# Attention and routed experts: k^T v turned once beside its logits' columns with orders made for it, and the second expert's second lot gathered in quarters and turned on VectorE

## The chip, the core and the metric

The kernel runs on one core of one Trainium2 chip. The metric is the device time of one execution in microseconds (us). A core has five engines that the text names: PE (TensorE, matrix products; its weight loads are listed as PEld), DVE (VectorE), ACT (ScalarE), POOL (GpSimd), and SP (SyncE, which here only issues transfers). Each engine works through its own instructions in order. 16 DMA engines move the data.

## What is computed

Linear attention per head, a norm over each head's 64 values, and then a mixture of 8 experts in which each token goes to one. B = H = 8, S = 576 tokens, D = 64, so 4608 tokens of 512 values; each expert has 1024 hidden values. All in fp32.

```python
kv  = einsum('bhsd,bhse->bhde', k, v)            # 64 x 64 per batch and head
out = einsum('bhsd,bhde->bhse', q, kv)
x   = out / sqrt(mean(out*out, -1) + 1e-6) * g_norm      # then B, S, 512
logits = x @ w_gate;  local = sigmoid(x @ w_local)
for each batch b, token s:
    e = argmax(logits[b, s]) if s == 0 or local[b, s] < 0.5 else prev_e
    prev_e = e
    p = exp(logits - max) / (sum + 1e-9)
    y[b, s] = p[e] * (relu(x[b, s] @ w1[e]) @ w2[e])
```

A token's expert can so depend on the token before it, and how many tokens an expert has is known only on the chip.

## The kernel before

**Attention part.** 16 steps, four groups of two batches by four pairs of heads. Step i loads q, forms q times kv for its pair (`q_kv`, L456), forms k^T v for step i+2 (`kv`, L375), and prepares the operand for step i+1. The numbers x have three users: the experts, the norm's sums, and the routing logits. The logits are not taken from x: kv times the gate's weights (9 columns a head: 8 experts and the local gate) is appended to kv, so that one product gives the 64 outputs and the 9 logits of a head. For that, k^T v has to be turned (`turn_kv`, L406), multiplied by the gate's weights `gw` (`logits_of`, L422) and copied in beside kv. Tiles: `kvp` is a pair's k^T v, copied out of PSUM by ACT; `kq` is its turned form; `kvb` is the operand for q, a block for each head laid beside a block of zeros, written by four POOL copies of 64x128 (`kvb_of`, L396) and, for the logits, by two ACT copies. The raw outputs (`raw`, 128x584 a chunk) are stored to a DRAM tile `xs` in rows of four quarters: 128 values, two reciprocal norms and the routing numbers, 146 in each.

A step's work is written as letters that a loop turns into code: `STEP` for the ordinary step and `LATE` for the last three. Q and R are the parts of `q_kv`, K and k those of `kv` of step i+2, V is `turn_kv` of step i+2, L and l the product and copy of the logits of step i+1, 0 and 1 the `kvb` copies, T and U the turns of q, a and c the copies of `raw`, x y X Y the squares for the norm, s the sums, o the store of a chunk (with a weight load in the steps of `LOADED`), w and v the split of a weight (steps of `SPLIT`), e the loads of q. `SLOTS` and `PASS` place the pieces of the routing among them. Inside these parts the order on PE, ACT, DVE and POOL is the order of the code.

**Precision.** Products of the experts are made from numbers split in two: a high part (`w_..h`, `xh`, `hh`) by ACT, a rest (`w_..l`, `xl`, `hl`) by DVE, and three matmuls. A weight tile `wst` (512 KB, four buffers) is loaded by SP (`wfetch`, issued at L186), split by `wsplit` (ACT L233, where the norm's weight is multiplied in, then DVE L234), and the split's end issues the load of the next one in the list.

**Experts.** They are ranked by how many tokens they have. Rank 0 is worked in four blocks of 128 tokens; its fourth block (`block(...)`, L1351) has the splits of rank 1's four w1 tiles (`split`, `w_4` to `w_7`) at its hooks 2, 4, 7 and 8, among its own relu (L1075) and casts (L1082) on ACT. Behind it follow the scales (`scale`, L808) and turns of rank 1's first lot. Ranks 1 to 7 have room for 768, 704, 640, 608, 608, 576 and 512 tokens, each in two lots: `la` of 384 and `lb` of the rest. A lot's first layer is `first_wide` (PE ph, ACT hh L1031, DVE hl L1032), its second is `second` by blocks of 128 (PE py, ACT ot L996, and a POOL scatter of the results at L997).

**Two ways to gather.** Rank 1 fetches each block of 128 tokens with one indirect transfer of whole rows (`gather`, L770, index tile `gidr`), scales it on DVE and turns it on PE (`turn`, L820, four transposes, with an ACT cast and a DVE subtraction behind, L824 and L825). Ranks 2 to 7 fetch a block with four indirect transfers of a quarter row each (`gather4`, L780, index tile `gid4`), partition quarter by partition quarter in such a way that 32x32 transposes on DVE (`turn4`, L797, with L801 and L802 behind) are enough. The rows of w1 then have to be loaded in the order of the quarters (`quarters` in `wfetch`, `gq` in place of `gcol` in the split), which `e > 1` chooses:

```python
if i < NW1 and quarters:
    fetch(t, w1[e].rearrange("o (q j i) f -> j (o q) i f", j=NP, i=QD)[i])
elif i < NW1:
    fetch(t, w1[e, i * P:(i + 1) * P, :].rearrange("o p f -> (o p) f"))
```

The lots' gathers are issued on POOL one after another in the order of the code: rank 1's second lot behind the fourth block's scatter (L1369, `lb`), those of a later lot by `tick` between the products of the lot before it.

Of the kernel before, what the change touches and what calls it, by code (L numbers as in the profile page):

```python
# [22 lines left out]
def kernel(  # L23
# [12 lines left out]
    nc = tc.nc  # L36
# [73 lines left out]
    gid4 = const.tile([P, NP, NR * KBM - KBM], I32, name="gid4")  # L110
# [89 lines left out]
    def wload(e, i):  # L200
        t = wpools["w"].tile([P, 2 * DM], F32, name="wst", bufs=4)
        wfetch(t, by[e], i, e > 1)
        staged[e, i] = t
# [36 lines left out]
    def wsplit(e, i, two=False):  # L240
# [9 lines left out]
        low_ = split_w(hi, lo, t, i, e > 1)  # L250
# [115 lines left out]
    def kv(s):  # L366


        pk = ps_o.tile([P, 2, 512], F32, name="po")
        ks, vs = ([t.pop((s, b)) for b in range(2)] for t in (kts, vts))  # L370
        for c in range(C):
            cd = slice(c * D, (c + 1) * D)
            for b in range(2):
                for x in range(2):
                    nc.tensor.matmul(pk[half(x ^ b), x, 0:D], ks[b][half(x), cd],  # L375
                                     vs[b][half(x), cd], start=(c == 0), stop=(c == C - 1))
        yield
        kvps[s] = wk.tile([P, 2, D], F32, name="kvp")
        nc.scalar.copy(kvps[s], pk[:, :, 0:D])  # L379
        yield  # L380
# [10 lines left out]
    def kvb_of(s, t):  # L391

        if s not in kvbs:
            kvbs[s] = wk.tile([P, 2 * HW + 2 * (HW + D)], F32, name="kvb", bufs=3)
        for y in range(2):
            copy[KVB[t]](pair(kvbs[s][half(t)], slot(0, y) + XO, slot(1, 1 - y), D),  # L396
                         kvps[s][half(y)])
# [3 lines left out]
    def turn_kv(s):  # L401

        pt = ps_q.tile([P, 2, P], F32, name="pt", tag="pq")
        kvp = kvps[s].rearrange("p x d -> p (x d)")
        for t in range(2):
            nc.tensor.transpose(pt[:, 0:2, half(t)], kvp, ident)  # L406
        kqs[s] = wk.tile([P, 2, P], F32, name="kq", bufs=3)
# [10 lines left out]
    def logits_of(s):  # L418

        pm = ps_q.tile([P, 2, 2 * NG], F32, name="pm", tag="pq")  # L420
        for y in range(2):
            nc.tensor.matmul(pm[:, y], kqs[s][:, y], gw[:, s % NP], start=True, stop=True)  # L422
        yield
        for y in range(2):
            copy[LGC](pair(kvbs[s], slot(0, y), slot(1, 1 - y) + D, NG),
                      pm[:, y].rearrange("p (x e) -> p x e", x=2))
# [223 lines left out]
    def by_quarter():  # L650

        n = NR * KBM - KBM
        pq4 = rbank[:, 128:128 + NP * n].rearrange("p (u n) -> p u n", n=n)
        for u in range(NP):
            nc.tensor.matmul(pq4[:, u], sel[0][:, u], trs[0][:, KBM:], start=True, stop=True)
# [122 lines left out]
    def gather4(xr, c, u):  # L778
# [4 lines left out]
            in_offset=bass.IndirectOffsetOnAxis(ap=gid4[:, u, c - KBM:c - KBM + 1], axis=0),  # L783
# [31 lines left out]
    def turn(xr, xh, xl, t0, psum, tag="pt", pin=False, late=False):  # L815

        pt = psum.tile([P, ND, P], F32, name="pt", tag=tag)
        xv = pieces(xr)
# [21 lines left out]
    LOADED = {i: j for j, i in enumerate((0, 1, 2, 3, 5, 10, 13, 14))}  # L840
    SPLIT = {i: j for j, i in enumerate((2, 4, 6, 8, 11, 12, 15))}

    STEP = "Q0saKcwkopRTq1vLlYVmUxeb"
    LATE = {NST - 3: "QKsw1vqkcabLRpo0mlGTVYXUe", NST - 2: "QcmKkLpTRoUea20qlV13xbsy", NST - 1: "45sQRwvacOyX"}

    SLOTS = {}
    for g in range(NGRP - 1):
        for x, what in enumerate("m pqb mb qq p qq".split()
                                 if g < NGRP - 2 else "q . pppmm".split()):
# [9 lines left out]
    def work_of(i, what):  # L859
# [14 lines left out]
        elif what == "R" and now:  # L874
            next(step["c"])
        elif what in "ac" and now:
            next(step[what])
# [261 lines left out]
    PASS = dict(at.split(":") for at in "a0:22o2 a2:s a4:223 a6:3 b1:33t b3:o c3:3x c4:3 c6:T3 d0:3z d5:3 d6:3f d7:r3 d11:3 d15:yF3l".split())  # L1139
# [153 lines left out]

    class Block:
# [17 lines left out]
        def scale(self):  # L1312
            scale(self.xr)
# [10 lines left out]
        def turn(self, xh, xl, t0):  # L1324
            if self.whole:
                turn(self.xr, xh, xl, t0, ps_t)
# [6 lines left out]
    def parts(r):  # L1333
# [3 lines left out]
        bl = [Block(r, k, min(P, n - k * P), r == 1) for k in range(-(-n // P))]  # L1337
# [30 lines left out]
    with tc.manual_schedule(engines=order):  # L1368
        for bl in lb:  # L1369
            bl.gather()  # L1370
# [92 lines left out]
```

## Time and profile before

| what | value |
|---|---|
| median of 3 timed runs | 580.54 us (579.57 to 580.59) |
| profiled execution, its own time | 575.91 us |
| its span, from first to last instruction | 574.1 us |
| DMA traffic | 94.96 MB, 165 GB/s over the span |
| mean granted clock of TensorE | 0.98 |
| largest group on POOL, the quarter gathers (L780) | 120, 133.5 us busy, 1112 ns each |
| weight loads on SP (512 KB each) | 64, median 3.7 us from issue to landing |
| whole-row gathers of rank 1 (L770, `gidr`) | 6, median 6.6 us from issue to landing |

The profile is of one execution. Its busy times are averages over very different parts: attention with the transfers of q, k, v and `xs`, about 9 to 124 us; the four blocks of rank 0, about 124 to 178 us; then ranks 1 to 7 to the end. Rows of the trace show start, duration, engine, line, what is written and read, and in brackets the idle time before it and what ended that. The profiled execution is 4.6 us shorter than the median of the timed runs.

### The profile page before, as it was taken

The page shows a single profiled execution, that of the slowest core. Times are in us where ns is not written, and L with a number is a line of the kernel's source. Part 1 is how long each engine was busy: PE and PEld are TensorE (multiplying, and loading weights), DVE is VectorE, ACT ScalarE, POOL GpSimd, SP SyncE. Part 2 cuts the span into 40 slices and gives each one's busy share as a digit, 9 for nine tenths or more (in the row PEclk, how much of TensorE's full clock was granted, in tenths as well). Part 3 has the DMA queues.
Part 4 walks back from the last instruction along what each step waited for, and adds up shares of the span by engine and source line. Part 5 has one row for each costly group of instructions (what it writes and reads, how often), then busy time and mean ns, then how long its engine had stood idle before and what let it go on. Part 6 is the DMA issues. An engine that isn't in the chain of part 4 may idle for free. (4 is left out here: it accounts for less than half of the span.)

```text
span 574.1 us, 12792 instructions
## 1 busy us (share of the span) xinstructions
PE 538.0 (94%) x5157; PEld 481.0 (84%) x5157; DVE 303.2 (53%) x627; ACT 237.6 (41%) x435; POOL 232.1 (40%) x303
## 2 busy tenths in 40 slices
PE   2977987789999999999999999999999999999996
PEld 2866876679878989898898898989798979999894
DVE  1126676699686525635463746374536545564510
ACT  1667766572254233332434343433433333435220
POOL 4224333161245527334353673447344634532001
PEclk9989889799999999999999999999999999999998
DMA  7999899980676354233343453336234533432000
GB/s 222 342 372 341 306 324 348 346 293 25 239 254 219 122 180 134 71 103 103 120 117 120 128 139 109 126 123 176 80 135 134 142 104 132 135 105 78 18 20 30
DMA packets 41379, 94.96 MB, mean 165 GB/s; under 512 B 7263, under 2 KB 7263, under 8 KB 41312
## 3 DMA queue, kind: packets, MB, share of 16 engines
q1 hardware_dynamic: 32032, 72.64, 37.1%
q0 software_dynamic: 7744, 21.41, 12.5%
q8 instruction: 42, 0.69, 0.5%
q10 hardware_dynamic: 1536, 0.02, 0.1%
q14 instruction: 25, 0.20, 0.1%
HBM read 73.85 MB, written 20.86 MB: 165 GB/s over the span
## 5 line engine op out<-in xcount | busy, mean ns | idle before, releaser
L780 POOL DMA_INDIRECT xr<-xs,gid x120 | 133.5, 1112 | 36.6 <-issue 33.2
L1032 DVE SCALAR_TENSOR_TENSOR hl<-ph,hh 128x384 fp32r<-128x384 f32 (+3 forms) x92 | 52.3, 569 | 113.6 <-ACT hh L1031 110.2
L997 POOL DMA_INDIRECT out_dram<-ot,sidr x34 | 33.8, 994 | 176.1 <-ACT ot L996 134.1
L1031 ACT ACTIVATE hh<-ph 128x384 fp32r<-128x384 f32 (+3 forms) x92 | 46.9, 510 | 121.7 <-PE ph L967 121.7
L996 ACT ACTIVATE ot<-py,pe 128x512 f32<-128x512 f32 (+1 forms) x37 | 25.4, 687 | 70.1 <-PE py L967 31.6
L495 POOL TENSOR_TENSOR sq<-raw 128x576 f32<-128x576 f32 x16 | 18.5, 1159 | 58.4 <-ACT raw L465 51.5
L375 PE MATMUL po<-vt,kt 64*64 64x64 f32 x1152 | 26.1, 243 | 15.7 <-DMA vt<-in_v_dram 11.5
L375 PEld LDWEIGHTS po<-vt,kt 64*64 64x64 f32 x1152 | 23.8, 156 | 14.3 <-issue 9.7
L500 DVE TENSOR_REDUCE ms<-sq 128x9 f32<-128x576 f32 x32 | 22.8, 747 | 21.5 <-POOL sq L495 19.5
L456 PEld LDWEIGHTS po<-kvb,qT 64*64 64x64 f32 x1024 | 22.2, 144 | 11.6 <-issue 9.3
L456 PE MATMUL po<-kvb,qT 64*64 64x73 f32 x1024 | 27.3, 242 | 4.7 <-issue 4.6
L462 ACT COPY raw<-po 128x876 f32<-128x876 f32 (+1 forms) x32 | 20.7, 651 | 15.3 <-PE po L456 15.1
L396 POOL COPY kvb<-kvp 64x128 f32<-64x128 f32 x64 | 20.5, 321 | 12.4 <-ACT kvp L379 10.0
L808 DVE TENSOR_TENSOR xr<-xr 128x512 f32<-128x512 f32 x37 | 25.4, 686 | 0.0
L801 ACT CAST yh<-xT 128x512 fp32r<-128x512 f32 x17 | 10.5, 620 | 29.5 <-DVE xT L797 29.4
L961 PE MATMUL py<-w_1h,hh 128*128 128x512 f32 (+1 forms) x56 | 22.2, 397 | 0.0
L435 PE MATMUL pq<-ident,qt 128*128 128x128 f32 x128 | 20.4, 307 | 1.8 <-issue 1.7
L966 PE MATMUL py<-w_0l,hh 128*128 128x512 f32 (+1 forms) x56 | 22.1, 395 | 0.0
L967 PE MATMUL py<-w_0h,hl 128*128 128x512 f32 (+1 forms) x56 | 22.0, 393 | 0.1
L961 PE MATMUL py<-w_0h,hh 128*128 128x512 f32 (+1 forms) x56 | 22.0, 393 | 0.0
L966 PE MATMUL py<-w_1l,hh 128*128 128x512 f32 (+1 forms) x56 | 21.9, 391 | 0.0
L967 PE MATMUL py<-w_1h,hl 128*128 128x512 f32 (+1 forms) x56 | 21.9, 391 | 0.0
(433 smaller groups left out, 1660.2 us busy)
## 6 DMA issues: line engine op xcount, KB each, us to landing
wst<-in_moe_w_dram SPq DMA_DIRECT2D x64, 512.0 KB, 3.7
xs<-raw SPq DMA_DIRECT2D x36, 292.0 KB, 4.4
kt<-in_k_dram SPq DMA_DIRECT2D x32, 288.0 KB, 4.6
vt<-in_v_dram SPq DMA_DIRECT2D x32, 288.0 KB, 4.9
qt<-in_q_dram SPq DMA_DIRECT2D x32, 288.0 KB, 5.5
xr<-xs,gid POOLq DMA_INDIRECT x120, 4.3
out_dram<-ot,sidr POOLq DMA_INDIRECT x36, 4.4
xr<-xs,gidr POOLq DMA_INDIRECT x6, 6.6
```

The costliest lines, as they stand in the source:

```text
L375: nc.tensor.matmul(pk[half(x ^ b), x, 0:D], ks[b][half(x), cd], vs[b][half(x), cd], start=(c == 0), stop=(c == C - 1))
L456: nc.tensor.matmul(po[half(b), r, o:o + HW], lhsT[half(r), half(x)], kvb[half(r), slot(x, b):slot(x, b) + HW], start=True, stop=True)
L500: nc.vector.tensor_reduce(mss[g][:, :, 2 * n + x], sqs.pop((s, x)), axis=AX.X, op=ALU.add)
L780: i = nc.gpsimd.indirect_dma_start(out=xr[:, u * PW:(u + 1) * PW], out_offset=None, in_=xs.rearrange("t (q w) -> (t q) w", w=PW), in_offse ...
L808: (engine or nc.vector).tensor_mul(xv, xv, r.unsqueeze(3).to_broadcast([P, NP, 2, D]))
L961: mm = nc.tensor.matmul(ps, ah, bh, start=(first and i == 0), stop=False)
L966: nc.tensor.matmul(ps, ah, bl, start=False, stop=False)
L967: nc.tensor.matmul(ps, al, bh, start=False, stop=(last and i == n - 1))
L996: nc.scalar.activation(ot[0:m], po[0:m], AF.Copy, scale=pe[0:m])
L997: return nc.gpsimd.indirect_dma_start(out=outf, out_offset=bass.IndirectOffsetOnAxis(ap=idx[0:m], axis=0), in_=ot[0:m], in_offset=None, bo ...
L1031: nc.scalar.activation(hh, ps, AF.Relu)
L1032: nc.vector.scalar_tensor_tensor(hl, ps[:, :, 0:nl], 0.0, hh[:, :, 0:nl].bitcast(F32), op0=ALU.max, op1=ALU.subtract)
```

## The change

There are two parts, and orders made anew for the first.

**k^T v.** `kvp` becomes a tile of 146 columns: the logits of head 0, kv of both heads, the logits of head 1. `turn_kv` makes one transpose of 128x128 where it made two, `logits_of` one product of 18 columns where it made two, and one ACT copy, into `kvp`. The `kvb` copies move kv and the logits together, 146 columns, so they come behind the logits (`assert s in lgs`). `STEP`, `LATE`, `LOADED`, `SPLIT`, `SLOTS` and `PASS` are written anew.

**The second expert (rank 1).** Its second lot is gathered in quarters and turned by `turn4`, as later ranks are. Its w1 must then be in the order of the quarters (`e > 0`). Its first lot is still gathered in whole rows and turned on PE; the new `scale_turned` writes the scaled values with the columns in that same order. `gid4` has three columns more a quarter.

```diff
@@ -199,7 +199,7 @@
     def wload(e, i):
         t = wpools["w"].tile([P, 2 * DM], F32, name="wst", bufs=4)
-        wfetch(t, by[e], i, e > 1)
+        wfetch(t, by[e], i, e > 0)
...
-        low_ = split_w(hi, lo, t, i, e > 1)
+        low_ = split_w(hi, lo, t, i, e > 0)
...
-        kvps[s] = wk.tile([P, 2, D], F32, name="kvp")
-        nc.scalar.copy(kvps[s], pk[:, :, 0:D])
+        kvps[s] = wk.tile([P, 2 * (HW + D)], F32, name="kvp")
+        nc.scalar.copy(kvps[s][:, XO:XO + 2 * D].rearrange("p (x d) -> p x d", x=2), pk[:, :, 0:D])
...
     def kvb_of(s, t):
 
+        assert s in lgs
         if s not in kvbs:
-            kvbs[s] = wk.tile([P, 2 * HW + 2 * (HW + D)], F32, name="kvb", bufs=3)
+            kvbs[s] = wk.tile([P, 4 * HW], F32, name="kvb", bufs=3)
         for y in range(2):
-            copy[KVB[t]](pair(kvbs[s][half(t)], slot(0, y) + XO, slot(1, 1 - y), D),
-                         kvps[s][half(y)])
+            copy[KVB[t]](kvbs[s][half(t), slot(0, y):slot(0, y) + 2 * HW],
+                         kvps[s][half(y), 0:2 * HW])
...
     def turn_kv(s):
 
-        pt = ps_q.tile([P, 2, P], F32, name="pt", tag="pq")
-        kvp = kvps[s].rearrange("p x d -> p (x d)")
-        for t in range(2):
-            nc.tensor.transpose(pt[:, 0:2, half(t)], kvp, ident)
-        kqs[s] = wk.tile([P, 2, P], F32, name="kq", bufs=3)
+        pt = ps_q.tile([P, P], F32, name="pt", tag="pq")
+        nc.tensor.transpose(pt, kvps[s][:, XO:XO + 2 * D], ident)
+        kqs[s] = wk.tile([P, P], F32, name="kq", bufs=3)
         nc.scalar.copy(kqs[s], pt)
...
     def logits_of(s):
 
-        pm = ps_q.tile([P, 2, 2 * NG], F32, name="pm", tag="pq")
-        for y in range(2):
-            nc.tensor.matmul(pm[:, y], kqs[s][:, y], gw[:, s % NP], start=True, stop=True)
+        pm = ps_q.tile([P, 2, NG], F32, name="pm", tag="pq")
+        nc.tensor.matmul(pm.rearrange("p x e -> p (x e)"), kqs[s], gw[:, s % NP],
+                         start=True, stop=True)
         yield
-        for y in range(2):
-            copy[LGC](pair(kvbs[s], slot(0, y), slot(1, 1 - y) + D, NG),
-                      pm[:, y].rearrange("p (x e) -> p x e", x=2))
+        copy[LGC](pair(kvps[s], 0, HW + D, NG), pm)
+        lgs.add(s)
         yield
...
-    LOADED = {i: j for j, i in enumerate((0, 1, 2, 3, 5, 10, 13, 14))}
...
-    STEP = "Q0saKcwkopRTq1vLlYVmUxeb"
...
+    LOADED = {i: j for j, i in enumerate((-2, -1, 1, 3, 5, 9, 12, 14))}
...
+    STEP = "QLwKsaRl0k1ocqTvmUpVebxY"
...
+    def scale_turned(xr):
+
+        t = xtile(xp, XB)
+        tv = t[:, 0:DM].rearrange("p (x y a i) -> p x a y i", x=2, a=NP, i=QD)
+        xv = pieces(xr).rearrange("p a (x y i) -> p x a y i", x=2, i=QD)
+        r = pieces(xr, XR, 2)
+        for x in range(2):
+            nc.vector.tensor_mul(tv[:, x], xv[:, x], r[:, :, x:x + 1].unsqueeze(3).to_broadcast(
+                [P, NP, DM // P // 2, QD]))
+        return t[:, 0:DM].rearrange("p (d k) -> p d k", k=P)
+
...
         def scale(self):
-            scale(self.xr)
+            if self.whole:
+                self.xs = scale_turned(self.xr)
+            else:
+                scale(self.xr)
...
-        bl = [Block(r, k, min(P, n - k * P), r == 1) for k in range(-(-n // P))]
+        bl = [Block(r, k, min(P, n - k * P),
+                    r == 1 and k < na // P) for k in range(-(-n // P))]
...
         for bl in lb:
-            bl.gather()
+            for what in bl.gathers():
+                what()
```

What stands on the engines can be read from their programs. First SP, in the first rows behind the stores of the attention part: the four loads of rank 1's w1 (`wst`), each behind a register instruction (ISA) that sets the expert's address. Before:

```order
L186 DMA wst<-in_moe_w_dram 128x2x512
L186 DMA xs<-raw 128x584 x15
L1122 TENSOR_LOAD cnt
L1122 ISA x14
L186 ISA
L186 DMA wst<-in_moe_w_dram 128x1024
```

After:

```order
L186 DMA wst<-in_moe_w_dram 128x2x512
L186 DMA xs<-raw 128x584 x18
L1124 TENSOR_LOAD cnt
L1124 ISA x14
L186 ISA
L186 DMA wst<-in_moe_w_dram 128x1x1024
```

The four loads keep their place; their form is now the one of the quarters, which before the change first stood in rank 2. Three stores of `xs` stand behind the last weight load of rank 0 that stood ahead of it.

Next ACT, in rank 0's fourth block, the program between the third block's results and rank 1's first layer. Before (`w_4h` to `w_7h` are the high parts of rank 1's w1, `h` and `hh` belong to the block):

```order
L233 ACTIVATE w_4h<-wst,gcol 128x1024
L1075 ACTIVATE h<-ph 128x512
L233 ACTIVATE w_5h<-wst,gcol 128x1024
L1082 CAST hh<-pt 128x4x128
L233 ACTIVATE w_6h<-wst,gcol 128x1024
L1075 ACTIVATE h<-ph 128x512
L233 ACTIVATE w_7h<-wst,gcol 128x1024
L1082 CAST hh<-pt 128x4x128
L824 CAST xh<-pt 128x4x128 x3
```

After:

```order
L233 ACTIVATE w_4h<-wst,gq 128x1024
L1077 ACTIVATE h<-ph 128x512
L233 ACTIVATE w_5h<-wst,gq 128x1024
L1084 CAST hh<-pt 128x4x128
L233 ACTIVATE w_6h<-wst,gq 128x1024
L1077 ACTIVATE h<-ph 128x512
L233 ACTIVATE w_7h<-wst,gq 128x1024
L1084 CAST hh<-pt 128x4x128
L824 CAST xh<-pt 128x4x128 x3
```

Nothing moved here; the norm's weight comes in the order of the quarters (`gq`), and each split waits for a load of the other form.

Last POOL, from the gather of rank 0's fourth block (the first row) to the scatters of rank 1's second lot (the last). Before:

```order
L770 DMA xr_3040<-xs,gidx 128x584
L997 DMA out_dram<-ot,si_2802 4608x512
L770 DMA xr<-xs,gidr 128x584 x6
L997 DMA out_dram<-ot,sidx 4608x512
L780 DMA xr<-xs,gid_88 128x146 x10
L997 DMA out_dram<-ot,sidr 4608x512
L780 DMA xr<-xs,gid_88 128x146 x2
L997 DMA out_dram<-ot,sidr 4608x512 x2
```

After:

```order
L770 DMA xr_3108<-xs,gidx 128x584
L999 DMA out_dram<-ot,si_2754 4608x512
L770 DMA xr<-xs,gidr 128x584 x3
L999 DMA out_dram<-ot,sidx 4608x512
L780 DMA xr<-xs,gid_88 128x146 x22
L999 DMA out_dram<-ot,sidr 4608x512
L780 DMA xr<-xs,gid_88 128x146 x2
L999 DMA out_dram<-ot,sidr 4608x512 x2
```

Three whole-row gathers are gone from ahead of the fourth block's scatter (`sidx`), and twelve quarter gathers stand behind it, ahead of the ten of rank 2's first lot.

25 lines of the change are left out of this document (14 added, 11 removed).

## Prediction

> **What bounds the kernel now.** I read the page first, then the table of stretches, the queue of SP, and the time lines of ACT, DVE, PE and POOL around the places that the change touches.
>
> ```profile
> span 574.1 us, 12792 instructions
> PE 538.0 (94%) x5157; PEld 481.0 (84%) x5157; DVE 303.2 (53%) x627; ACT 237.6 (41%) x435; POOL 232.1 (40%) x303
> ```
>
> The share of PE alone says "TensorE bound"; the stretches say where that holds. Columns: busy time of PE, PEld, DVE, ACT and POOL, then the granted clock, the DMA share and GB/s.
>
> ```profile
> core 0: us, PE busy (x) PEld busy (x) DVE busy (x) ACT busy (x) POOL busy (x), PEclk, DMA share, GB/s
> 9.00:114.00 105.00, 84.82 (x2427) 76.25 (x2422) 52.69 (x120) 67.58 (x173) 32.96 (x73) 0.90 0.98 338
> 114.00:124.00 10.00, 8.28 (x179) 6.64 (x176) 9.47 (x30) 8.01 (x19) 6.07 (x10) 1.00 0.82 250
> 124.00:178.40 54.40, 53.42 (x339) 44.74 (x338) 44.65 (x122) 20.51 (x33) 17.93 (x16) 1.00 0.60 214
> 178.40:569.80 391.40, 390.42 (x2203) 352.43 (x2203) 194.76 (x350) 141.54 (x212) 169.17 (x156) 1.00 0.36 111
> ```
>
> The attention part (9 to 114 us) keeps the DMA engines busy 98% of the time while PE has 20 us to spare: it is bound by transfers. From 124 on, PE is busy all but about 2 us of 446. So an edit in the first stretch pays only through fewer bytes or fewer DMA gaps, and in the rest a saved PE instruction pays in full, unless a new wait stops PE.
>
> **The attention part (term A).** A step held this on PE (two logits products, two transposes, the next):
>
> ```profile
> 48.27 0.52 PE L422 MATMUL pm<-gw,kq 128*128 128x18 f32 x4
> 48.67 0.44 PE L406 MATMUL pt<-ident,kvp 128*128 128x128 f32 x2
> 49.16 0.44 PE L414 MATMUL pl<-ident,qt 128*128 128x128 f32 x2
> ```
>
> From 48.27 to 49.16 is 0.89 us; half of both goes, 0.45 us a step, 16 steps, 7 us of PE. One logits copy (ACT) of two goes as well. None of this moves a byte, so the 98% DMA share hides it; without that cover it would be worth up to 7 us. What is added:
>
> ```profile
> L396 POOL COPY kvb<-kvp 64x128 f32<-64x128 f32 x64 | 20.5, 321 | 12.4 <-ACT kvp L379 10.0
> ```
>
> These 64 POOL copies grow from 128 to 146 columns: between 321 ns and 321 x 146/128 = 366 ns each, at most 2.9 us in all, on an engine that is idle 72 of these 105 us. They also wait for the logits now (PE, then ACT, then POOL, then PE's next step); behind them on POOL stand the squares, and for those wait DVE's sums. Such a chain is about 0.9 + 0.25 + 4 x 0.33 = 2.5 us, estimated from ACT's copies and these rows, inside a step of 105/16 = 6.6 us. Two 512 KB weight loads are queued earlier and the seventh before the last q: the same bytes. I take **A = -0.5 us**. The DMA share leaves 2% of 105 us, 2.1 us, and something of the start, so -3 at best; a loaded q that comes 1.5 us later (512 KB at 338 GB/s) sets +1.5.
>
> **The second expert's first-layer weights (term B).** The diff turns `e > 1` into `e > 0` in two places, so that the four w1 loads of the expert of rank 1 take the form that the later experts use. That form's price stands in the trace. The issues on SP's queue (min/median/max ns, first and last start): of rank 1, and of rank 2, whose loads have the new form already:
>
> ```profile
> L186 SPq DMA_DIRECT2D wst<-in_moe_w_dram x4: 332/354/379, 160.3 to 162.0; - x4
> ...
> L186 SPq DMA_DIRECT2D wst<-in_moe_w_dram x4: 532/540/736, 183.4 to 189.7; - x4
> ```
>
> The stretches after both (columns as above):
>
> ```profile
> 164.00:168.00 4.00, 4.00 (x21) 3.29 (x21) 3.15 (x12) 3.06 (x5) 2.95 (x3) 1.00 0.98 387
> 184.00:199.00 15.00, 15.00 (x84) 14.32 (x83) 9.78 (x19) 5.58 (x10) 9.76 (x8) 1.00 0.38 112
> 199.00:204.00 5.00, 5.00 (x26) 4.09 (x25) 1.01 (x2) 1.27 (x2) 1.27 (x2) 1.00 0.26 102
> ```
>
> The old form fills the DMA engines (0.98, 387 GB/s) and is through in some 6 us. After the last of the four new-form loads was issued (189.7), the engines stay at 0.26 and 102 GB/s for many microseconds: a quarter of them work. Four loads of 524,288 bytes at 102 GB/s are 20.6 us. In rank 2 nobody notices, since these weights are wanted 20 us later. In rank 1 they are on the path. [...]
>
> Now who waits. ACT before the change:
>
> ```profile
> 164.36 1.15 ACT L233 ACTIVATE w_4h<-wst,gcol 128x1024 fp32r<-128x1024 f32 x1 [0.20 <-issue]
> 166.16 0.60 ACT L1075 ACTIVATE h<-ph 128x512 f32<-128x512 f32 x1 [0.65 <-PE ph L967]
> 166.65 1.15 ACT L233 ACTIVATE w_5h<-wst,gcol 128x1024 fp32r<-128x1024 f32 x1
> 167.90 0.59 ACT L1082 CAST hh<-pt 128x512 fp32r<-128x512 f32 x1
> 168.38 1.15 ACT L233 ACTIVATE w_6h<-wst,gcol 128x1024 fp32r<-128x1024 f32 x1
> 169.44 0.58 ACT L1075 ACTIVATE h<-ph 128x512 f32<-128x512 f32 x1
> 169.91 1.15 ACT L233 ACTIVATE w_7h<-wst,gcol 128x1024 fp32r<-128x1024 f32 x1
> 171.45 0.59 ACT L1082 CAST hh<-pt 128x512 fp32r<-128x512 f32 x1 [0.39 <-PE pt L1080]
> ```
>
> The four splits w_4h to w_7h are interleaved with the relu and the casts of expert 0's fourth block, and the order is unchanged. When a split waits for its load, the block's `h` and `hh` wait behind it on ACT, and PE waits for them. DVE goes on from there:
>
> ```profile
> 171.09 1.29 DVE L234 SCALAR_TENSOR_TENSOR w_7l<-wst,gcol,w_7h 128x1024 fp32r<-128x1024 f32 x1 [0.18 <-ACT w_7h L233]
> 172.29 0.68 DVE L1083 TENSOR_TENSOR hl<-pt,hh 128x512 fp32r<-128x512 f32 x1
> 172.90 0.68 DVE L808 TENSOR_TENSOR xr<-xr 128x512 f32<-128x512 f32 x1
> ...
> 177.63 0.69 DVE L825 TENSOR_TENSOR xl<-pt,xh 128x512 fp32r<-128x512 f32 x1 [0.52 <-ACT xh L824]
> ```
>
> and PE:
>
> ```profile
> 178.38 0.44 PE L966 MATMUL ph<-xl,w_4h 128*128 128x384 f32 x1 [0.29 <-DVE xl L825]
> ```
>
> w_7l, hl, three scales with turns, and PE's first wide layer at 178.38 follow w_7h by a fixed chain of 8.5 us. So the shift of the end is the shift of w_7h. The loads start to flow at about 161.5 (1.2 us after the first issue). Their four-of-sixteen engines also carry a quarter of three row gathers (4 x 73 KB of 128 x 2,336 bytes each, the six below cut to three) and of a 262 KB store of results:
>
> ```profile
> L770 POOL DMA_INDIRECT xr<-xs,gidr x6: 994/1172/1493, 165.7 to 173.6; - x6
> ```
>
> (2.10 + 0.22 + 0.06) MB at 102 GB/s is 23.3 us: the fourth load lands at 184.8, the first three at about 167, 173 and 179. w_7h moves from 169.91 to 184.8, +14.9 us. The scale of the three first-lot blocks is now two products of 128x256 with 32-element runs instead of one of 128x512; between twice 0.41 (a 128x252 product of the routing) and twice 0.68 against 0.68, so +0.14 to +0.68 a block. I take 0.14, as the size decides; three in the chain are +0.4. Low end: flow from 161.0 at 106 GB/s without other traffic, 19.8 us, 180.8, +11. High end: 162 and 25 us, 187, +17, and a cold PE on top:
>
> ```profile
> 35.00:39.00 4.00, 3.83 (x40) 3.58 (x39) 0.67 (x2) 2.06 (x6) 1.72 (x4) 0.57 1.01 382
> ```
>
> After a gap of 2.4 us the granted clock was 0.57 for 4 us here; gaps of 2 to 4 us return in the fourth block. DVE's chain covers most of it, up to 1.5 us may show. **B = +15.3 us, from +11 to +18.5.**
>
> **The second lot (term C).** Three blocks lose their turn on PE:
>
> ```profile
> 197.38 0.60 PE L820 MATMUL pt<-ident,xr 128*128 128x128 f32 x4
> 197.73 0.48 PE L961 MATMUL py<-w_5h,hh 128*128 128x512 f32 x1
> ```
>
> 0.35 us each, -1.05 us on a full PE. In exchange 12 quarter gathers replace three, ahead of rank 2's first ten, where those stood (the first and the last of the ten; then what the trace says of their landing; then DVE):
>
> ```profile
> 179.99 1.03 POOL L780 DMA_INDIRECT xr<-xs,gid  x1 [0.30 <-issue]
> ...
> 194.74 1.16 POOL L780 DMA_INDIRECT xr<-xs,gid  x1 [0.30 <-issue]
> ```
>
> ```profile
> DMA to landing us min/median/max: 7.7/7.9/8.2
> ```
>
> ```profile
> 194.34 0.68 DVE L808 TENSOR_TENSOR xr<-xr 128x512 f32<-128x512 f32 x1
> ...
> 195.99 0.56 DVE L1032 SCALAR_TENSOR_TENSOR hl<-ph,hh 128x384 fp32r<-128x384 f32 x1 [0.69 <-ACT hh L1031]
> ```
>
> Ten take 179.99 to 195.9, the twelfth would start at 197.3; they land about 8 us after their issue. On the clock of before, the second block's quarters (the eighth, issued at 192.1) are there at 200, and its scale is due at 194.34. DVE is in order: the last `hl` of the first lot waits behind that scale until 202, and PE wants it at 200.7, +1.2. The third block is there at 205.3; its scale stands ahead of the first turn, and ACT's cast of that turn ahead of the first results' copy out of PSUM, which holds the third block's products back by some 0.6 us more. The three turns end at 212.8, about when PE asks. With gathers that land in 4.3 us (the page's median) nothing waits and C is -1.05; if ten gathers more ahead of the first result store also hold its buffer, +3. I take **C = +0.75 us**.
>
> Sum: -0.5 + 15.3 + 0.75 = +15.5 us. The profiled execution took 575.9 us in all, 1.8 beside its span, and would take 591.4. The three timed runs have their median 4.6 us higher, at 580.5; I add the sum to the median: **596.0 us**.
>
> **The rivals.** (1) The loads are hidden after all: they use all engines because little else runs. The point is 169.9: the fourth has to land by then, 2.1 MB in 8.4 us, 250 GB/s. Then quarter gathers land early too, and A and C remain: -0.5 + 0.4 - 1.05 = -1.2, with a better front down to -3.5: 577 to 579.4, faster. For it: 387 GB/s in the old form. Against it: 0.26 with four loads in the queue. 6%. (2) Each load takes another quarter of the engines, so four at once fill them; all land at about 167. Then w_4h comes 2.5 us later, ACT catches up half of it in its gaps, and the end is 582. Against it: the same 0.26. 5%. (3) The 22 gathers in a row hold the first store of results, and its PSUM copy, until PE stands still for three blocks: C becomes +5 to +8, 600 to 603. For it: POOL is in order and its rows are 1.3 to 2.1 us apart. Against it: three PSUM tiles of slack. 9%. (4) The change doesn't do what it says (the second lot still turned on PE): excluded by PE's order.
>
> **How the numbers follow.** 80% for the forecast, 6, 5 and 9% for the rivals. The range takes in B's bounds with the middle of A and C, and part of the third rival: 588.5 to 601.5. A measurement of this kernel can tell 0.2%, 1.2 us, from no change. Faster: 5% of the first rival's 6. Within: 2% from the first two. Slower: 93%.
>
> **What would show it.** In the profile after: DMA share near 0.25 with extra gather peaks from 162 to 184 and no stretch of 390 GB/s; ACT's w_4h to w_7h some 5 to 6 us apart, each behind "DMA wst"; PE idle two to four times between 167 and 186; the first wide layer of rank 1 at about 193; DVE's last `hl` of the first lot behind a scale that waits for a gather. The prediction is wrong if w_7h starts before 175, or if the stretch from 9 to 114 shortens by more than 3 us.

## The result, and the profile after

The changed kernel takes 608.09 us (median of 4 runs, 604.55 to 608.63) against 580.06 us before (4 runs): 4.2% slower, ratio 1.0424 with a 95% interval of 1.0337 to 1.0511. That is +28.0 us by the medians and +24.6 by the ratio, where +15.5 was forecast, and both are above the forecast range. The profiled execution took 604.55 us, its span 602.7. (Ratios in this document leave out runs more than 1.5% above the fastest run of the same kernel, so for a kernel whose runs scatter a ratio can lie below that of the medians; the changed kernel's rests on four of its six recorded runs, 598.80 to 607.65 us.)

The head of the page of the changed kernel:

```profile
span 602.7 us, 12694 instructions
PE 546.9 (91%) x5097; PEld 484.5 (80%) x5097; DVE 304.4 (50%) x636; ACT 234.2 (39%) x419; POOL 247.9 (41%) x312
```

PE does 60 matmuls fewer and is busy 8.9 us longer. Three marks cut the 28.6 us of span into pieces. The first is the start of the first hidden values of rank 0 (`hh`, ACT), at 127.13 before; the second the split of rank 1's fourth w1 tile (`w_7h`), at 169.91 before; the third the end. ACT after the change:

```profile
136.05 0.60 ACT L1033 ACTIVATE hh<-ph 128x512 fp32r<-128x512 f32 x1 [1.02 <-PE ph L969]
...
178.80 1.15 ACT L233 ACTIVATE w_4h<-wst,gq 128x1024 fp32r<-128x1024 f32 x1 [5.58 <-DMA wst<-in_moe_w_dram]
179.85 0.58 ACT L1077 ACTIVATE h<-ph 128x512 f32<-128x512 f32 x1
187.46 1.15 ACT L233 ACTIVATE w_5h<-wst,gq 128x1024 fp32r<-128x1024 f32 x1 [7.03 <-DMA wst<-in_moe_w_dram]
...
194.79 1.15 ACT L233 ACTIVATE w_6h<-wst,gq 128x1024 fp32r<-128x1024 f32 x1 [5.71 <-DMA wst<-in_moe_w_dram]
...
199.81 1.15 ACT L233 ACTIVATE w_7h<-wst,gq 128x1024 fp32r<-128x1024 f32 x1 [3.40 <-DMA wst<-in_moe_w_dram]
```

Up to the first mark +8.9 us (the attention part); from there to the second 63.8 us instead of 42.8, so +21.0 (the weights); from there to the end 402.9 instead of 404.2, so -1.3. Each of the four splits now waits for its load, as the prediction had it, and they stand 5 to 9 us apart. The stretches (columns as in the prediction):

```profile
169.00:170.00 1.00, 0.81 (x4) 0.34 (x2) 0.97 (x4) 0.00 (x0) 0.00 (x0) 1.00 0.00 0
170.00:171.00 1.00, 0.87 (x9) 0.90 (x9) 0.03 (x1) 0.20 (x1) 0.00 (x0) 1.00 0.17 12
171.00:172.00 1.00, 1.00 (x9) 0.92 (x9) 0.58 (x1) 0.38 (x1) 0.00 (x0) 1.00 0.12 41
172.00:173.00 1.00, 1.00 (x6) 0.80 (x5) 0.93 (x7) 0.47 (x1) 0.00 (x0) 1.00 0.23 78
173.00:174.00 1.00, 1.00 (x6) 0.83 (x5) 0.86 (x6) 0.22 (x1) 0.50 (x1) 1.00 0.26 94
174.00:175.00 1.00, 1.00 (x6) 0.80 (x6) 0.90 (x5) 0.00 (x0) 0.69 (x2) 1.00 0.26 102
...
180.00:190.00 10.00, 4.08 (x12) 2.61 (x12) 2.62 (x3) 2.05 (x3) 0.00 (x0) 0.72 0.44 144
190.00:200.00 10.00, 5.96 (x15) 3.74 (x14) 1.81 (x2) 1.82 (x3) 0.00 (x0) 0.50 0.57 157
```

The loads were issued from 169.31 on. Up to 175 the DMA share stays at 0.26 or under; later it is higher (0.44 and 0.57 on average), where gathers and the next loads are under way as well. PE is busy 10 of the 20 us, at a granted clock of 0.72 and then 0.50.

### The profile page after: what moved, and what is told of

Its sections match the earlier page's. It is cut to its first block, busy times and chain, and to the rows that moved or that the text cites. A ratio compares the mean times of both kernels' runs of the same rounds, so it can differ in the third digit from the quotient of the medians.

```text
span 602.7 us, 12694 instructions
## 1 busy us (share of the span) xinstructions
PE 546.9 (91%) x5097; PEld 484.5 (80%) x5097; DVE 304.4 (50%) x636; ACT 234.2 (39%) x419; POOL 247.9 (41%) x312
## 5 line engine op out<-in xcount | busy, mean ns | idle before, releaser
L780 POOL DMA_INDIRECT xr<-xs,gid x132 | 147.3, 1116 | 42.1 <-issue 38.8
L397 POOL COPY kvb<-kvp 64x146 f32<-64x146 f32 x64 | 23.3, 365 | 59.7 <-ACT kvp L425 51.3
L456 PE MATMUL po<-kvb,qT 64*64 64x73 f32 x1024 | 32.6, 250 | 11.6 <-issue 10.9
L456 PEld LDWEIGHTS po<-kvb,qT 64*64 64x64 f32 x1024 | 25.8, 151 | 17.3 <-issue 13.6
L375 PE MATMUL po<-vt,kt 64*64 64x64 f32 x1152 | 25.3, 241 | 14.3 <-DMA vt<-in_v_dram 7.4
L375 PEld LDWEIGHTS po<-vt,kt 64*64 64x64 f32 x1152 | 22.3, 153 | 15.4 <-issue 13.0
L801 ACT CAST yh<-xT 128x512 fp32r<-128x512 f32 x20 | 12.4, 620 | 40.9 <-DVE xT L797 40.8
L808 DVE TENSOR_TENSOR xr<-xr 128x512 f32<-128x512 f32 x34 | 23.4, 687 | 7.1 <-DMA xr<-xs,gid 7.1
L797 DVE STREAM_TRANSPOSE xT<-xr 128x512 f32<-128x512 f32 x33 | 23.3, 707 | 0.5
```

The source lines that it names most:

```text
L397: copy[KVB[t]](kvbs[s][half(t), slot(0, y):slot(0, y) + 2 * HW], kvps[s][half(y), 0:2 * HW])
L456: nc.tensor.matmul(po[half(b), r, o:o + HW], lhsT[half(r), half(x)], kvb[half(r), slot(x, b):slot(x, b) + HW], start=True, stop=True)
L780: i = nc.gpsimd.indirect_dma_start(out=xr[:, u * PW:(u + 1) * PW], out_offset=None, in_=xs.rearrange("t (q w) -> (t q) w", w=PW), in_offse ...
L797: nc.vector.transpose(xT.rearrange("p j (u k) -> p u j k", k=QD), pieces(xr).rearrange("p u (j i) -> p u j i", i=QD))
L808: (engine or nc.vector).tensor_mul(xv, xv, r.unsqueeze(3).to_broadcast([P, NP, 2, D]))
```

## The experiments

Sixteen kernels ran, in four groups on three chips, each compared with the kernel before on its own chip. The scatter of the kernel before differs from chip to chip (573 to 580, 580 to 594, 576 to 585 and 576 to 584 us in the four groups), so ratios are compared, and behind the first mark the profiles, which there repeat to 1 us where a chip is quiet.

| kernel | ratio (95% interval) | median, and of before (us) |
|---|---|---|
| e1_front | 1.0125 (1.0077 to 1.0173) | 585.43, 578.43 |
| e2_rank | 1.0345 (1.0290 to 1.0400) | 599.66, 578.43 |
| e3_after16 | 1.0221 (1.0166 to 1.0277) | 589.60, 578.43 |
| e4_rank16 | 1.0135 (1.0082 to 1.0188) | 584.17, 578.43 |
| e5_loads | 1.0175 (1.0120 to 1.0229) | 595.79, 585.72 |
| e6_code | 1.0066 (1.0011 to 1.0121) | 592.14, 585.72 |
| e7_order | 1.0161 (1.0105 to 1.0217) | 595.20, 585.72 |
| e8_hold | 1.0404 (1.0327 to 1.0480) | 610.40, 585.72 |
| e9_front64 | 1.0029 (0.9982 to 1.0076) | 585.68, 580.23 |
| e10_before64 | 0.9998 (0.9958 to 1.0038) | 580.80, 580.23 |
| e11_before32 | 1.0027 (0.9985 to 1.0069) | 582.54, 580.23 |
| e12_hold | 1.0322 (1.0252 to 1.0392) | 598.38, 580.23 |
| e13_five | 1.0065 (1.0031 to 1.0099) | 583.81, 580.35 |
| e14_lean | 1.0056 (1.0015 to 1.0097) | 583.51, 580.35 |
| e15_code | 1.0113 (1.0065 to 1.0161) | 585.02, 580.35 |
| e16_order | 1.0214 (1.0162 to 1.0266) | 591.50, 580.35 |

### The two parts apart

e1_front takes rank 1's part out of the changed kernel; e2_rank puts that part alone into the kernel before.

```diff
# e1_front, against the changed kernel
-        wfetch(t, by[e], i, e > 0)
+        wfetch(t, by[e], i, e > 1)
... (the split, the scale and the gathers go back in the same way)
-                    r == 1 and k < na // P) for k in range(-(-n // P))]
+                    r == 1) for k in range(-(-n // P))]
```

> Only the attention part of the change (k^T v turned once, the new orders, kvb copied behind the logits); rank 1 is gathered, loaded and turned as before. Theory from the trace of the changed kernel, where the first hidden values of rank 0 come at 136.05 instead of 127.13: this part costs 9 us by itself, 589 +- 2 (1.015). Rival, the prediction's term A: between -3 and +1.5 us, 577.5 to 582; then the 9 us of the one profiled run were chance, and the second expert would have to cost all 28.

> Only the second expert's part (quarter gathers and turn on VectorE for its second lot, first-layer weights in the order of the quarters, scale_turned); the attention part is that of before. Theory from the trace: the split of the fourth weight comes 20.9 us later than the front explains, and 0.9 us come back behind it, so +20, 600 +- 2. Rival, the prediction's terms B and C: +16, 596.5. Rival, the attention part is innocent: +28, 608.

Measured: +7.0 and +21.2 us in the medians, together 28.2 of the 28.0; by the ratios it is 7.2 and 20.0 us, together 27.1 against 24.6. Within the scatter the parts add up, and both cost. (e1_front stayed under its 589 +- 2 and above the rival's 582.) In the profiles e1_front has its first mark at 141.09 and then 446.1 us to the end (before: 447.0): behind the attention part it is the kernel before. e2_rank has 64.2 us from the first mark to `w_7h`, as the changed kernel (63.8).

### The form of the weight loads

```diff
# e3_after16 and e4_rank16, for rank 1
-                fetch(t, w1[e].rearrange("o (q j i) f -> j (o q) i f", j=NP, i=QD)[i])
+                    rows = w1[e].rearrange("o (q j i) f -> q j (o i) f", j=NP, i=QD)
+                    for u in range(NP):
+                        fetch(t[u * QD:(u + 1) * QD], rows[u, i])
```

> The changed kernel, but each of rank 1's four first-layer weight tiles is loaded by four transfers of 32 partitions (one for each quarter) instead of one transfer of four quarters. If the cost of the second expert's part is that such a load runs on 4 of 16 DMA engines: the DMA share behind the first issue is near 1 again, the four splits follow each other as before the change, and of the 28 us some 20 go; 16 issues of 0.57 us each delay the fourth load by some 1.5 us, so 588 to 591. Rival, the gathers or the order of the engines hold the block: 600 or more.

> The kernel before with the second expert's part alone, its first-layer weights loaded by four transfers of 32 partitions each. Theory: 0.4 (scale_turned) + 1.5 (16 issues) - 0.9 (no turn on PE) = +1, 581 to 582; if the issues are hidden, 579.5. Rival, the late quarter gathers cost the +0.75 of the prediction's term C: 582.5 to 583.5.

From the first mark to the end it is 450.0 us in e3_after16's profile and 451.6 in e4_rank16's, against 446.1 in e1_front's, 447.0 before, and 466.6 and 467.5 with the loads in one piece. So 16 to 17 of the 20 us hang on the form of these four loads alone. The stretches of e4_rank16, the first one before the row gathers (issued from 167.91 on):

```profile
164.00:166.00 2.00, 2.00 (x13) 1.74 (x13) 1.43 (x6) 0.85 (x2) 0.00 (x0) 1.00 0.85 232
...
168.00:172.00 4.00, 3.50 (x19) 2.62 (x18) 2.21 (x4) 3.22 (x4) 3.13 (x3) 1.00 0.92 275
172.00:176.00 4.00, 1.81 (x7) 0.84 (x5) 1.07 (x3) 1.19 (x2) 0.00 (x0) 1.00 1.04 267
```

The DMA engines are busy again: a share of 0.85 with the loads alone, where one piece had 0.26, and 0.92 to 1.04 with the gathers beside them. 3 to 4.6 us stay, more than the 1 expected (e4_rank16's 584.17 us is above its theory and its rival). The 16 issues take from 162.5 to 171.1 us, where the four of before went out within 1.7 us, so the later loads run beside the row gathers and the next tile's load (issued at 172.3); which of these holds them is not shown. ACT's fourth split stands 48.9 us behind that profile's first mark (129.18) instead of 42.8:

```profile
178.07 1.15 ACT L238 ACTIVATE w_7h<-wst,gq 128x1024 fp32r<-128x1024 f32 x1 [1.63 <-DMA wst<-in_moe_w_dram]
```

### What else the four engines carry

Of the 21 us the forecast had 14.9. Each split's end issues the next load in the list, rank 1's w2, and by the reckoning of the prediction a quarter of that falls on the same four engines; its sum had left that out. (Four is the author's estimate from the share of 0.26 of 16; no profile here tells the engines apart.)

```diff
# e12_hold, against e2_rank
+        if e == 1 and i == NW1 - 1:
+            fourth_in_.append(fetched[-1])
+        if e == 1 and NW1 <= i < NW1 + 3:
+            tc.add_manual_dep(fetched[-1].ins, fourth_in_[0].ins.name, ...)
```

> The second expert's part alone (as e2_rank), but the loads that the splits of rank 1's first three w1 tiles issue (rank 1's w2) are held until its fourth split. Theory: three loads put 131 KB each on the same four DMA engines, 3 x 131 KB at 102 GB/s = 3.9 us; without them the fourth split comes about 4 us earlier counted from rank 0's first hidden values (before 64.3 us in e2_rank's profile, then 60 to 61), and the time is about 596. Rival, the loads alone run at less than 102 GB/s because of the row gathers: the split stays at 63 to 65 us.

> The second expert's part alone (as e2_rank), where the loads of rank 1's w2 wait on SP until its fourth w1 load has landed. The held loads in the run before this one stood in the same place of SP's program and went out at the same times, so it told nothing; here they wait for the landing. Theory: three of these loads put 131 KB each on the four DMA engines that the w1 loads use, 3.9 us; from rank 0's first hidden values to the split of the fourth tile it takes 60 to 61 us instead of 64.3. Rival, the w1 loads alone are that slow: 63 to 65.

e8_hold moved only the place in the code where the loads are asked for. SP's program stayed the same, and a load left whenever its buffer came free (at 181.4, 190.5 and 195.8, in e2_rank 181.6, 189.7 and 195.3), so it tested nothing; 63.2 us from mark to mark. e12_hold makes the loads wait for the landing. ACT there (first mark 129.35, first load issued at 162.43):

```profile
172.44 1.15 ACT L239 ACTIVATE w_4h<-wst,gq 128x1024 fp32r<-128x1024 f32 x1 [6.16 <-DMA wst<-in_moe_w_dram]
...
180.64 1.15 ACT L239 ACTIVATE w_5h<-wst,gq 128x1024 fp32r<-128x1024 f32 x1 [6.58 <-DMA wst<-in_moe_w_dram]
...
185.72 1.15 ACT L239 ACTIVATE w_6h<-wst,gq 128x1024 fp32r<-128x1024 f32 x1 [3.46 <-DMA wst<-in_moe_w_dram]
...
190.80 1.15 ACT L239 ACTIVATE w_7h<-wst,gq 128x1024 fp32r<-128x1024 f32 x1 [3.45 <-DMA wst<-in_moe_w_dram]
```

From the first mark to `w_7h` it takes 61.45 us, 1.8 to 2.8 less than in the three kernels without the hold (63.8, 64.2 and e8_hold's 63.2). The shift has the sign of the theory and about half to three quarters of its 3.9 us; it rests on one profile, and those without the hold differ by 1.0 among themselves. The time does not tell (1.0322 against 1.0345, intervals overlap). The rows give the price of the form: with no gather and no other load under way (DMA share 0.25 and 102 GB/s from 181 to 183; 0.2 and 91 GB/s in the page's slice from 178.5 to 193.4) a load takes 5.08 us (185.72 to 190.80), 524,288 bytes at 103 GB/s. The first came 10.0 us after its issue and the second 8.2 us after the first, while three row gathers ran.

### The attention part

In e1_front and the changed kernel the DMA engines run dry, that is, have almost nothing to move, at 44 to 47 us (e1_front: shares of 0.14, 0.05 and 0.00 in the three microseconds). The changed kernel there:

```profile
44.00:47.00 3.00, 1.39 (x52) 1.30 (x52) 0.00 (x0) 0.51 (x2) 0.41 (x2) 1.00 0.08 22
```

That gave the first theory: weight loads that moved.

```diff
# e5_loads, against e1_front
-    LOADED = {i: j for j, i in enumerate((-2, -1, 1, 3, 5, 9, 12, 14))}
-    SPLIT = {i: j for j, i in enumerate((2, 4, 6, 8, 11, 13, 15))}
+    LOADED = {i: j for j, i in enumerate((0, 1, 2, 3, 5, 10, 13, 14))}
+    SPLIT = {i: j for j, i in enumerate((2, 4, 6, 8, 11, 12, 15))}
```

> The attention part alone (as e1_front), with the steps of the weight loads and splits as before the change; all else of the new orders stays. In the three profiles with the new orders the DMA engines run dry at 44 to 47 us, where a k load waits 5 us for PE's product of the step (PE po L375) and no weight load stands ahead of it; in the old order one does. If that is the cost: no dry stretch there, and 4 of the 7 us go, 581 to 582. Rival, it lies at the tail or in the code of the k^T v part: 585 to 586 as e1_front.

Nothing came back (1.0175), and the engines run dry at 44 to 47 us all the same (share 0.28), so the places of the weight loads are not what empties them: this theory falls. Code and orders apart, each twice (e6_code and e15_code: the new code with before's `STEP`, `LATE`, `SLOTS`, `PASS`, loads and splits, L and l put ahead of the `kvb` copies; e7_order and e16_order: the old code with the new ones):

```diff
# e6_code and e15_code, against e1_front (with before's LOADED, SPLIT, SLOTS and PASS)
-    STEP = "QLwKsaRl0k1ocqTvmUpVebxY"
+    STEP = "QLl0saKRwkopcTq1vYVmUxeb"
# e7_order and e16_order, against before (with the new LOADED, SPLIT, LATE, SLOTS and PASS)
-    STEP = "Q0saKcwkopRTq1vLlYVmUxeb"
+    STEP = "QLwKsaRl0k1ocqTvmUpVebxY"
```

> The attention part's new code (one transpose, one logits product, one copy into kvp, kvb copied behind the logits) in the orders of before: same loads, splits, routing places and letters, only L and l put ahead of the kvb copies, since the new code needs that. If the orders cost the 7 us: 577 to 580, no change. Rival, the code costs them (kvb copies that wait for the logits, 146 columns on POOL): 584 to 587.

> The old code (two transposes, two logits products, two copies into kvb, kvb copied from kv alone) in the new orders, loads, splits and routing places. If the orders cost the 7 us: 584 to 587, a little more than e1_front at most. Rival, the code costs them: 577 to 580.

> e6_code once more (new code of the attention part in the orders of before). It gave 1.0066 with runs from 583 to 601 us on a chip that scattered. Orders cost all: 0.998 to 1.003. Code costs all: 1.010 to 1.014. Both: in between.

> e7_order once more (old code of the attention part in the new orders). It gave 1.0161. Orders cost all: 1.010 to 1.018. Code costs all: 0.998 to 1.003.

On the quieter chip the code alone costs 1.0113 and the orders alone 1.0214, together (e1_front, e14_lean) 1.0056 to 1.0125. So both cost, and the orders cost less with the code that they were made for (1.0056 against 1.0214 on one chip). Neither of the two theories, that one of them costs all, holds.

Second theory: PE stands still at many of the places where another 127 or so products are done, and the profile names nothing that ended the wait (it writes `issue` there); where these stops fall decides. PE after the change:

```profile
112.65 0.85 PE L456 MATMUL po<-kvb,qT 64*64 64x73 f32 x36 [0.43 <-issue]
113.44 0.40 PE L422 MATMUL pm<-gw,kq 128*128 128x18 f32 x2
113.76 1.28 PE L375 MATMUL po<-vt,kt 64*64 64x64 f32 x72
114.97 0.56 PE L723 MATMUL rbank<-ab,lo 128*128 128x96 bf16 x9
115.46 0.36 PE L456 MATMUL po<-kvb,qT 64*64 64x73 f32 x8
117.76 0.36 PE L456 MATMUL po<-kvb,qT 64*64 64x73 f32 x8 [1.94 <-issue]
```

From one stop to the next there are 36 + 2 + 72 + 9 + 8 = 127 products, 254 instructions with their weight loads. In before's trace there are 127 products, 127 weight loads and two semaphore instructions, 256 in all, from behind the stop that ends at 29.80 us to the end of the next, at 35.17. Tiny products ahead of the first shift the places:

```diff
# e9_front64 (on e1_front), e10_before64 and, with 32, e11_before32
+    pad = ps_q.tile([P, P], F32, name="pad", tag="pq")
+    for _ in range(64):
+        nc.tensor.matmul(pad[0:32, 0:8], iota_l[:, 0:32], iota_l[:, 0:8], start=True, stop=True)
```

> The attention part alone (as e1_front) with 64 tiny matmuls put ahead of PE's first product (128 instructions, a half of the 256 after which PE stands still without a releaser; PE has nothing to do for 7 us there). Theory: the 7 us of the attention part are DMA engines that run dry because PE's stops fall into k^T v products, which hold the buffers of the next k loads; where the stops fall is a matter of the count of instructions. Then the dry stretch at 44 to 47 us goes or moves, and the time changes by 3 us or more from e1_front's 1.0125, to either side. Rival, the work or the chain of the new code costs them: 1.0125 +- 0.003 again.

> The kernel before with the same 64 tiny matmuls ahead of PE's first product. Theory: the place of PE's stops decides, so an unchanged attention part also changes by 3 us or more (more likely slower, as its stops fall well), with dry DMA stretches between 35 and 60 us. Rival: within 0.3% of before.

> The kernel before with 32 tiny matmuls ahead of PE's first product (a quarter of 256 instructions). Theory: another place of PE's stops, another time than both before and the one with 64, by 2 us or more from one of them. Rival: within 0.3% of before.

The kernel before does not care (0.9998 and 1.0027), though its stops fall elsewhere (e10_before64 has 6.6 us of them at L375 and 3.1 at L456, where before has 4.2 and 8.3), so with the old code the place of the stops does not decide. For the new code it stays open. In e9_front64 the dry stretch did move (to 56 to 60 us, with shares of 0.43, 0.07, 0.00 and 0.61), but its twelve runs lie between 577.2 and 590.8 us. The ratio, 1.0029, rests on the lower six; it cannot be told from before and is 1% under e1_front's, as the theory had it. The median of all twelve is 5.4 us above before's. The profile, with a late first mark (138.46), is of one of the upper six.

Third theory: the buffers through which PE's stops hold the transfers.

```diff
# e14_lean, against e1_front; e13_five has the last line as well
-            kvbs[s] = wk.tile([P, 4 * HW], F32, name="kvb", bufs=3)
+            kvbs[s] = wk.tile([P, 4 * HW], F32, name="kvb")
...
-        kqs[s] = wk.tile([P, P], F32, name="kq", bufs=3)
+        kqs[s] = wk.tile([P, P], F32, name="kq")
...
-    ld = right.enter_context(tc.tile_pool(name="ld", bufs=4, side="right", reuse_waits="tile"))
+    ld = right.enter_context(tc.tile_pool(name="ld", bufs=5, side="right", reuse_waits="tile"))
```

> The attention part alone (as e1_front), with five buffers each for k and v in place of four; to make room, kvb and kq have two buffers in place of three. The first k and v load of each step then waits for no product of PE. If the dry DMA stretches come from that wait: they shrink by up to 0.59 MB at 340 GB/s = 1.7 us each, and with two or three such stretches 3 to 5 of the 7 us go, 1.004 to 1.007 in ratio. Rival, PE's stops themselves are the cost and the dry DMA engines only follow: 1.012 as e1_front and e14_lean.

> Control of e13_five: the attention part alone with two buffers for kvb and kq, four for k and v. If these two buffers don't matter: 1.010 to 1.015, e1_front's again.

The stretch from 35 to 60 us, of e14_lean and then of e13_five:

```profile
35.00:60.00 25.00, 20.61 (x540) 17.84 (x530) 8.84 (x15) 14.23 (x37) 8.47 (x18) 0.80 0.74 257
```

```profile
35.00:60.00 25.00, 20.57 (x554) 17.49 (x558) 10.91 (x23) 16.70 (x42) 8.97 (x18) 0.93 0.92 321
```

With five buffers the DMA engines are busier there (0.92 instead of 0.74, 1.6 MB more moved), PE gets no further (20.6 us busy in both), and the time is the same. e13_five's 1.0065 is what its theory forecast, but the control has it too: e14_lean came out at 1.0056, not at the 1.010 to 1.015 expected, so the fifth buffer did not bring it. Whether two buffers for `kvb` and `kq` in place of three did is open (its interval overlaps e1_front's, from another chip). In this stretch the transfers follow PE and don't set its pace. The tables of waits below say the same of the rest: from 17 us to the first mark 0.8 us of PE's waits in the profile of before, and none in that of the changed kernel, end with a load.

What does differ is PE itself. All of the attention part in one row, from 9 us to the first mark, before and after:

```profile
9.00:127.13 118.13, 96.23 (x2635) 85.97 (x2629) 65.12 (x150) 78.26 (x197) 40.88 (x84) 0.91 0.97 332
```

```profile
9.00:136.05 127.05, 100.07 (x2563) 87.25 (x2558) 64.66 (x150) 74.80 (x180) 46.45 (x85) 0.89 0.92 314
```

and PE's longest waits in it, by the table of waits (us in total, times, longest), before and after; its stops are the rows with `issue`:

```profile
PE po L456 <- issue: 8.3, 5, 3.7
PE po L375 <- issue: 4.2, 3, 2.4
PE po L375 <- DMA vt<-in_v_dram: 3.5, 3, 1.5
PE pq L435 <- issue: 1.7, 1, 1.7
PE pm L422 <- issue: 1.5, 1, 1.5
```

```profile
PE po L456 <- issue: 10.9, 9, 2.5
PE po L375 <- issue: 7.0, 3, 3.5
PE pm L422 <- DVE gw L309: 3.7, 1, 3.7
PE pq L435 <- issue: 2.0, 1, 2.0
```

72 matmul records fewer, and PE is busy 3.8 us longer, at a lower granted clock (0.89 instead of 0.91); its stops are 19.9 us instead of 15.7. These two make 8.0 of the 8.9 us. The wait for `gw` at the start is new, but costs next to nothing: PE waited for v there before, and the first turn of q starts at 17.43 instead of 17.04 us. Over the profiles: the seven with the old attention part have 12.5 to 17.0 us of stops (mean 14.8) and the first mark at 127.1 to 136.4 (mean 131.3); nine with new code, new orders or both (without e6_code and e9_front64, profiled in runs that their ratios leave out) have 16.1 to 23.3 (mean 19.5) and 132.6 to 143.3 (mean 137.5). The mark is 6.1 us later, with 4.7 us more of stops and 2.7 more of busy PE.

What the stops are can be read from the transfers in the same traces, which time a queue named `instruction` (packets, MB, share). The whole of before's profile, then its PE row behind the longest stop (101.49 to 105.20), then that queue within the stop, from 102.9 to 104:

```profile
q8 instruction: 42, 0.69, 0.5%
```

```profile
105.20 0.75 PE L456 MATMUL po<-kvb,ql 64*64 64x73 f32 x8 [3.71 <-issue]
```

```profile
q8 instruction: 1, 0.02, 5.7%
```

It is a packet of 16,384 bytes, from 102.96 to 103.96, and PE goes on 1.24 us after it. So it is everywhere: in the eighteen profiles the attention part has 171 stops of 0.5 us or more, and each ends 1.15 to 1.62 us after such a packet has landed (in the profiles of before and of the changed kernel 20 of 20, 1.17 to 1.54 us). The profiles give the queue's name and the times and not what a packet holds; from these the author takes it that PE waits there for its next instructions.

None of the sixteen is faster than the kernel before, and none points to a version that would be.

## Why the prediction was wrong in size

**The direction and its main cause were right.** The forecast named the form of rank 1's first-layer loads, ACT's four splits behind them, and the block behind ACT. The late split at +21.0, its four waits, and the 16 to 17 us that go with another form show it. With transfers of 32 partitions (e4_rank16) the share is 0.85 for the loads alone, in place of 0.26. The rivals in which all engines or changing quarters carry a load are out: a load alone ran at 103 GB/s, and with all four issued (the last at 171.9) the share stayed at 0.23 to 0.26 from 172 to 175 us.

**Term B, +15.3 (up to 18.5), was 19.7 to 20.5 with C in it.** The shift of the fourth split was put at 14.9 and was 21.0. Reckoned from the first issue, the four splits were forecast at 6.7, 12.7, 18.7 and 24.5 us and came at 9.5, 18.1, 25.5 and 30.5. The step that failed is the division of bytes by 102 GB/s from 1.2 us after the first issue on. The flow had 12, 41 and 78 GB/s in its first three microseconds, and the first load came 2.8 us late. The second lost 2.7 more beside the three row gathers, for which 2.2 us in all had been counted. No run shows that a quarter of a gather or of a store falls on the loads' engines, as the 0.22 and 0.06 MB of the sum have it; what e12_hold shows is 10.0 and 8.2 us for the first two loads, beside three row gathers, and 5.08 for one alone. And the w2 loads, issued by the splits themselves, were not in the sum: 1.8 to 2.8 us by the run that held them. The cold clock, for which up to 1.5 stood in the upper bound, shows at most 0.2: from `w_7h` to the first hidden values of rank 1 it takes 10.9 us instead of 10.8.

**Term A, -0.5 (up to +1.5), was +8.9 in the profile and +7.0 in the medians of e1_front's runs.** The step that failed is "None of this moves a byte, so the 98% DMA share hides it". A DMA share of 98% was read as "bound by transfers"; with five buffers the transfers got ahead in the stretch looked at (0.92 instead of 0.74), and the time stayed (1.0065 and 1.0056). PE's stops, 15.7 us of the 118 before the change and 19.9 of the 127 after it, were not a term of the sum, nor was the clock behind them (0.50 from 105.2 to 110 us before, behind the stop of 3.7 us), so the 7 us of removed PE work were taken as a saving that waits under a cover. They were not a saving at all: PE was busy longer. And the upper bound had only the late load of q in it.

**Term C, +0.75, was about 0.** From `w_7h` to the end the four profiles with rank 1's part and no held loads are 1.0 to 1.7 us shorter than before's, but e1_front, without that part, is 1.0 shorter too. The scale did wait for its gather and the last `hl` stood behind it, as said, and PE was not stopped by it. Of the third rival, a result store behind a row of gathers, there is a small sign. ACT's copy of results waits 4.7 us for an earlier store to leave its buffer, the relu of the second lot's first layer stands behind it, and PE loses 0.5 us. ACT and PE of the changed kernel there:

```profile
246.89 0.69 ACT L998 ACTIVATE ot<-py,pe 128x512 f32<-128x512 f32 x1 [4.72 <-DMA out_dram<-ot,sidr]
```

```profile
248.61 0.44 PE L963 MATMUL ph<-yh,w_4h 128*128 128x384 f32 x1 [0.51 <-DVE hl L1034]
```

What stays open: why PE's stops are longer (a mean of 19.5 us instead of 14.8) with either the new code or the new orders. The places of the weight loads and the buffers of k and v are excluded as single causes, and for the old code the place of the stops; for the new code the place of the stops and the third buffer of `kvb` and `kq` are not. An experiment that changes the length of the stops directly was not made.

## What to carry to other kernels

A form of load that keeps few of the DMA engines busy (here a share of 0.26, where the other form had 0.98) was harmless in rank 2, where its data was wanted 20 us later, and cost its full time in rank 1, where it was wanted next: 5.08 us for a load alone, at 103 GB/s where 387 were moved in all with the other form. Before reusing a form, look at what stands between its issue and its use, and put into the sum everything that runs beside it, also the transfers that the waiting work itself will issue (holding these gave back 1.8 to 2.8 us here). A DMA share near 100% (0.98 here) does not by itself say that transfers set the pace; PE's own idle time for which the profile names no cause, and the clock behind it (15.7 us and 0.50 here), belong in the sum of such a stretch, and it pays to lay its ends beside the packets of the queue `instruction` (here 171 of 171 stops end behind one). And an order that is tuned to one version of the code can lose several microseconds with another version (e16_order: 591.50 us against 580.35).

## What the runs showed of the hardware

PE stopped at multiples of about 127 products (254 instructions with their weight loads, 256 with the two semaphore instructions between the stops at 29.80 and 35.17 us of before), for up to 3.7 us before the change, while the DMA engines were 92 to 97% busy in the profiles of the old part. In one attention part the stops are 12.5 to 23.3 us. That they end behind packets of the instruction queue is shown by their times (171 of 171); what sets the times of the packets is not shown. In the experts' part before, where 127 products take some 23 us (2203 in 391.40 us), 19 such packets come as well and PE has no such cost (busy 390.42 of 391.40 us).

The start of the loads in the order of the quarters was slow beside their rate alone (103 GB/s): 12, 41, 78 and then 94 and 102 GB/s in the first five microseconds from 170 us on, in the profile of the changed kernel.
